# Two layers of local attention and feed-forward: another engine for the second x tile's statistics, a second DMA ring for the first weights, and the V halos on another engine

## The chip, the cores and the metric

The kernel runs on one core of a Trainium2 chip. The metric is the time of one execution on the device in microseconds. Each kernel was run several times. Kernels are compared only within the same rounds. The span in a profile starts a little later and ends a little earlier than the timed execution: 1228.4 us against 1230.1 us for the profiled run of the kernel before.

## The reference, cut to what matters

Two layers, each a sliding attention (32 heads of 32, window 8 with dilation 2) and a feed-forward part, with a layer norm ahead of both. x has 2048 rows of 1024, wqkv is 1024 x 3072, everything is bf16.

```python
def _layernorm(x, axis=-1, eps=1e-5):
    m = jnp.mean(x, axis=axis, keepdims=True)
    v = jnp.var(x, axis=axis, keepdims=True)
    return (x - m) / jnp.sqrt(v + eps)
# _A_ref: qkv = x @ wqkv, local attention, @ wo      _B_ref: gelu(x @ w1 + b1) @ w2 + b2
x = A_x
x = x + _A_ref(_layernorm(x, axis=-1), A_wqkv, A_wo)
x = x + _B_ref(_layernorm(x, axis=-1), B_w1, B_b1, B_w2, B_b2)
x = x + _A_ref(_layernorm(x, axis=-1), A_wqkv, A_wo)
x = x + _B_ref(_layernorm(x, axis=-1), B_w1, B_b1, B_w2, B_b2)
```

Nothing can be multiplied before the first rows of x are loaded, normalised and transposed. That start is what the change is about.

## The kernel before

The rows are cut into 16 tiles of 128, and four tiles make a group. For the first group the kernel loads x tiles 0 and 1, then Wq in four pieces of 512 KB (two row blocks each, "quarters" below) with x tiles 2 and 3 in between, all issued by SyncE:

```python
    def load_wq_piece(wt, k):
        sp.dma_start(wt[:, k % (KD // 2):k % (KD // 2) + 2, :], wqkv_v[:, k:k + 2, 0:D])

    load_x(0, 0, 2)
    wq_first = [wpool.tile([P, KD // 2, D], BF16, name="wt") for _ in range(2)]
    for k in range(0, KD, 2):
        load_wq_piece(wq_first[k // (KD // 2)], k)
        if k < 4:
            load_x(0, 2 + k // 2, 3 + k // 2)
    # ...
    act.activation(one[:], eps_t[:], ACT.Sqrt)      # ScalarE's first activation, behind a table load
```

TensorE first runs 14 warm-up matmuls. Meanwhile VectorE computes the statistics of tiles 0 and 1 and ScalarE the square roots; then both tiles are normalised and transposed on TensorE. The last two lines put tiles 2 and 3 behind, in program order:

```python
        stats(0)
        stats(1)
        xn0 = norm(0)
        xn1 = norm(1, (0, 2 * P, D))
        transpose_on_pe(xn0, xa[0][:, 0, :, :], [(0, 2, act.copy), (2, 8, act.copy)])
        transpose_on_pe(xn1, xa[0][:, 1, :, :], [(0, 2, vec.tensor_copy)])
        transpose_on_pe(xn1, xa[0][:, 1, :, :], [(2, 8, act.copy)])
        stats(2)
        stats(3)
        for tt in range(2, 4):
            first_late.append((norm(tt), xa[0][:, tt, :, :]))
```

The first Wq matmuls then work on the columns of tiles 0 and 1 alone, a Wq quarter at a time, and the transposes of tiles 2 and 3 are slipped in:

```python
        for kq in range(4 if n == 0 else 0):
            for c in range(7):
                first[c] = qkv_chunk(wq, c, xnT, first.get(c), kq * (KD // 4), (kq + 1) * (KD // 4), 0, 2)
                if (kq, c) == (2, 3):
                    transpose_on_pe(*first_late.pop(0), [(0, KD, act.copy)])
                # ... tile 3 at (3, 4)
```

The halo of V (the last 14 columns of the group before) is copied by ScalarE, except in the second group:

```python
                (act.copy if n > 1 else pool.tensor_copy)(vT[:, :, 0:HALO], st[n - 1]["vT"][:, :, T:T + HALO])
```

## Time and profile before

| | kernel before |
|---|---|
| time, median of 3 runs | 1230.35 us (1230.22 to 1230.75) |
| span in the profile | 1228.36 us |
| TensorE busy | 99% |
| x1 landed | 4.25 us |
| first Wq matmul issued | 8.26 us |
| x3 landed | 9.91 us |
| transposes of tile 2 | 12.24 us |
| last weight load of TensorE | 1224.96 us |
| last output landed | 1227.38 us |

Times inside a run count from the start of the span. TensorE is busy 99% of the span, so only what happens before its unbroken run of matmuls starts, or a wait that breaks this run, or the end behind the last matmul, can change the time. The lines of the profile are shown in the prediction. To compare two kernels I use one more reading: each trace has the same 5770 weight loads of TensorE in the same order, so the start of the k-th load in one trace minus that in the other tells how far TensorE is behind at that point. Where this difference steps, time was lost or won.

### The profile page before, as it was taken

To read this page: it belongs to the slowest core of one execution; us is meant where nothing else is said; L and a number is where in the kernel's file an instruction comes from. 1 tells how busy PE (TensorE), PEld (TensorE's weight loads), DVE (VectorE), ACT (ScalarE), POOL (GpSimd) and SP (SyncE) were. 2 spreads that over 40 slices of the span, in tenths; PEclk is the share of its full clock that TensorE was granted. 3 is DMA by queue.
4 is the path that set the end of the run, shared out by engine and by line. 5 is a ranking of instruction groups with operands and counts; after the bars stand their busy time and mean duration, and the time that the engine had idled before them with its cause. 6 is when DMAs were issued, how large, how long until landed. Compare 5 with 4: busy or idle time off the path is not lost.

```text
span 1228.4 us, 13955 instructions
## 1 busy us (share of the span) xinstructions
PE 1221.6 (99%) x5720; PEld 632.7 (52%) x5770; DVE 861.5 (70%) x912; ACT 315.6 (26%) x497; POOL 120.9 (10%) x219
## 2 busy tenths in 40 slices
PE   9999999999999999999999999999999999999998
PEld 7666544456444564446544465444654444444444
DVE  7999896998898999375993759937599797011001
ACT  5343253014310233202431024410244001300310
POOL 2330025010101101100001000000000002000000
PEclk9999999999999999999999999999999999999999
DMA  9965674766638645856557565576664558446441
GB/s 302 290 206 164 176 233 151 202 178 199 219 128 245 188 150 166 239 170 175 161 158 230 172 171 181 157 216 201 171 200 147 186 194 209 149 159 194 156 135 52
DMA packets 223647, 226.64 MB, mean 185 GB/s; under 512 B 71824, under 2 KB 190752, under 8 KB 221536
## 3 DMA queue, kind: packets, MB, share of 16 engines
q1 hardware_dynamic: 214704, 208.69, 56.3%
q0 software_dynamic: 8880, 17.07, 4.2%
q8 instruction: 45, 0.74, 0.2%
q14 instruction: 18, 0.15, 0.0%
HBM read 189.01 MB, written 4.19 MB: 157 GB/s over the span
## 4 chain that ended last, share of the span: by engine, by line
PE 99%; DVE 0%; issue 0%; DMA 0%
PE acc L117 99%; DMA x<-in_A_x_dram 0%; DVE stats L92 0%; PE acc L211 0%; DVE xn L92 0%; DVE x L92 0%; DVE mv L92 0%; DVE rstd L92 0%
## 5 line engine op out<-in xcount | busy, mean ns | idle before, releaser
L117 PE MATMUL acc<-xnT,wt 128*128 128x512 bf16 (+1 forms) x3392 | 720.3, 375 | 0.1
L117 PEld LDWEIGHTS <-wt 128*128 128x128 bf16 x3392 | 400.8, 120 | 317.4
L117 PE MATMUL acc<-wt,hT 128*128 128x512 bf16 (+1 forms) x1780 | 386.0, 376 | 2.1
L117 PEld LDWEIGHTS <-hT 128*128 128x128 bf16 x1820 | 178.1, 98 | 209.0
L92 DVE TENSOR_TENSOR big<-big 128x1024 bf16<-128x1024 bf16 (+2 forms) x184 | 244.8, 1359 | 2.2
L92 ACT ACTIVATE hT<-acc,b1T 128x512 bf16<-128x512 f32 x224 | 152.1, 687 | 325.9 <-PE acc L117 325.8
L92 DVE TENSOR_TENSOR big<-qT,kT 128x4096 bf16<-128x4096 bf16 x64 | 143.8, 2283 | 36.3 <-ACT kT L92 35.9
L92 DVE TENSOR_TENSOR big<-abc,vT 128x4096 bf16<-128x4096 bf16 x64 | 144.6, 2284 | 11.0 <-DMA abc<-a 7.1
L92 DVE TENSOR_TENSOR tmp<-acc,b2bc 128x512 f32<-128x512 f32 x56 | 38.6, 689 | 159.8 <-PE acc L117 156.7
L92 ACT CAST qT<-acc 128x512 bf16<-128x512 f32 (+1 forms) x72 | 38.0, 543 | 276.8 <-PE acc L117 274.6
L117 PE MATMUL acc<-wt,oT 128*128 128x512 bf16 x440 | 97.6, 379 | 0.4
L92 DVE BATCH_NORM_STATS2 stats<-x 128x6 f32<-128x512 bf16 x116 | 77.4, 681 | 6.0 <-DMA x<-in_A_x_dram 5.0
L117 PEld LDWEIGHTS <-oT 128*128 128x128 bf16 x448 | 43.8, 98 | 53.0 <-issue 0.3
L92 DVE TENSOR_TENSOR x<-acc,big 128x512 bf16<-128x512 f32 (+1 forms) x9 | 5.7, 632 | 90.0 <-PE acc L117 90.0
L92 POOL TENSOR_TENSOR rstd<-mv,eps_t 128x1 f32<-128x1 f32 x54 | 16.7, 308 | 524.2 <-DVE mv L92 524.2
L92 ACT CAST vT<-acc 128x512 bf16<-128x512 f32 x64 | 37.4, 585 | 101.9 <-PE acc L117 101.9
L92 ACT CAST kT<-acc 128x512 bf16<-128x512 f32 x64 | 37.3, 584 | 64.5 <-PE acc L117 64.5
L92 DVE TENSOR_TENSOR x<-acc,x 128x512 bf16<-128x512 f32 x64 | 42.9, 670 | 5.1 <-PE acc L117 4.7
L92 DVE TENSOR_SCALAR xn<-x,mv,rstd 128x1024 bf16<-128x1024 bf16 (+2 forms) x53 | 28.5, 540 | 20.1 <-POOL rstd L92 19.9
L92 DVE TENSOR_TENSOR x<-tmp,x 128x512 bf16<-128x512 f32 x56 | 38.6, 689 | 1.4
L92 POOL DMA_DIRECT2D big<-big x24 | 13.3, 563 | 212.5 <-DVE big L92 212.5
L92 ACT ACT_TABLE_LOAD x17 | 21.8, 1283 | 38.9 <-DVE e L92 30.5
(62 smaller groups left out, 285.4 us busy)
## 6 DMA issues: line engine op xcount, KB each, us to landing
wt<-in_B_w_dram SPq DMA_DIRECT2D x56, 1024.0 KB, 5.6
wt<-in_B_w_dram SPq DMA_DIRECT2D x64, 896.0 KB, 4.8
wt<-in_A_wqkv_dram SPq DMA_DIRECT2D x46, 1024.0 KB, 5.6
wt<-in_A_wo_dram SPq DMA_DIRECT2D x16, 1024.0 KB, 5.0
abc<-a POOLq DMA_DIRECT2D x32, 256.0 KB, 4.6
big<-big POOLq DMA_DIRECT2D x24, 256.0 KB, 3.8
x<-in_A_x_dram SPq DMA_DIRECT2D x16, 256.0 KB, 7.1
out_dram<-x SPq DMA_DIRECT2D x31, 128.0 KB, 1.8
```

What stands on the lines that cost most here:

```text
L92: inst = f(*args, **kwargs)
L117: return pe(nc.tensor.matmul(*args, **kwargs))
```

## The change

Its intent is a shorter start. The statistics of x tile 1 go to ScalarE, so that VectorE can normalise tile 0 at once; its reciprocal square root goes to GpSimd. Wq comes in eight row blocks of 256 KB, three of them through ScalarE's DMA ring (the queue of the transfers that this engine issues), the rest through SyncE's; x tiles 2 and 3 are asked for one Wq quarter later. All V halos are copied by GpSimd. The loads:

```diff
-    def load_wq_piece(wt, k):
-        sp.dma_start(wt[:, k % (KD // 2):k % (KD // 2) + 2, :], wqkv_v[:, k:k + 2, 0:D])
+    def load_wq_piece(wt, k, engine):
+        engine.dma_start(wt[:, k % (KD // 2), :], wqkv_v[:, k, 0:D])
 
     load_x(0, 0, 2)
     wq_first = [wpool.tile([P, KD // 2, D], BF16, name="wt") for _ in range(2)]
     for k in range(0, KD, 2):
-        load_wq_piece(wq_first[k // (KD // 2)], k)
-        if k < 4:
-            load_x(0, 2 + k // 2, 3 + k // 2)
-
+        load_wq_piece(wq_first[k // (KD // 2)], k, sp)
+        if 2 <= k < 6:
+            load_x(0, 1 + k // 2, 2 + k // 2)
+
+    load_wq_piece(wq_first[1], KD - 1, sp)
 # ... cut
+    act.on = True
     act.activation(one[:], eps_t[:], ACT.Sqrt)
+    act.on = True
+    for k in range(1, KD - 2, 2):
+        load_wq_piece(wq_first[k // (KD // 2)], k, act)
+    act.on = False
```

The statistics and the halos:

```diff
+            if tt == 0:
+                rstds[tt] = lnp.tile([P, 1], F32, name="rstd")
+                pool.tensor_tensor(out=rstds[tt][:], in0=mvs[tt][:, 1:2], in1=eps_t[:], op=ALU.add)
+                pool.tensor_tensor(out=rstds[tt][:], in0=rstds[tt][:], in1=mhalf[:], op=ALU.pow)
+            else:
+                act.activation(stds[tt][:], mvs[tt][:, 1:2], ACT.Sqrt, bias=eps_t[:])
+
+        def stats_on_act(tt):
 # ... cut: junk, less, mvs[tt] are allocated
+            act.activation(junk[:], x[tt][:], ACT.Identity, scale=-1.0 / D, accum_out=less[:])
+            act.activation(junk[:], x[tt][:], ACT.Square, bias=less[:], accum_out=mvs[tt][:, 1:2])
+            act.activation(stds[tt][:], mvs[tt][:, 1:2], ACT.Sqrt, scale=1.0 / D, bias=eps_t[:])
 # ... cut
         stats(0)
-        stats(1)
+        less = stats_on_act(1)
         xn0 = norm(0)
+        vec.tensor_scalar(out=mvs[1][:, 0:1], in0=less[:], scalar1=-1.0, scalar2=None, op0=ALU.mult)
         xn1 = norm(1, (0, 2 * P, D))
 # ... cut
-                (act.copy if n > 1 else pool.tensor_copy)(vT[:, :, 0:HALO], st[n - 1]["vT"][:, :, T:T + HALO])
+                pool.tensor_copy(vT[:, :, 0:HALO], st[n - 1]["vT"][:, :, T:T + HALO])
```

More of the change, by code (lines that the diff above doesn't have):

```diff
@@ L228, in ln_first @@
         mvs = {}
-        stds = {}
+        stds, rstds = {}, {}
         def stats(tt):
@@ L237, in stats @@
             stds[tt] = lnp.tile([P, 1], F32, name="std")
-            act.activation(stds[tt][:], mvs[tt][:, 1:2], ACT.Sqrt, bias=eps_t[:])
+            if tt == 0:
[5 more added lines that the diff above has]
+        def stats_on_act(tt):
+            junk = lnp.tile([P, D], BF16, name="xn", bufs=3)
+            less = lnp.tile([P, 1], F32, name="less")
+            mvs[tt] = lnp.tile([P, 2], F32, name="mv")
+            act.activation(junk[:], x[tt][:], ACT.Identity, scale=-1.0 / D, accum_out=less[:])
+            act.activation(junk[:], x[tt][:], ACT.Square, bias=less[:], accum_out=mvs[tt][:, 1:2])
+            stds[tt] = lnp.tile([P, 1], F32, name="std")
+            act.activation(stds[tt][:], mvs[tt][:, 1:2], ACT.Sqrt, scale=1.0 / D, bias=eps_t[:])
+            return less
         def norm(tt, bounds=(0, D)):
-            rstd = lnp.tile([P, 1], F32, name="rstd")
-            vec.reciprocal(rstd[:], stds[tt][:])
+            rstd = rstds.get(tt)
+            if rstd is None:
+                rstd = lnp.tile([P, 1], F32, name="rstd")
+                vec.reciprocal(rstd[:], stds[tt][:])
             xn = lnp.tile([P, D], BF16, name="xn", bufs=3)
```

## The prediction

> **What bounds the kernel now.** I read the page first: busy time by engine, then the chain that ended last.
>
> ```profile
> PE 1221.6 (99%) x5720; PEld 632.7 (52%) x5770; DVE 861.5 (70%) x912; ACT 315.6 (26%) x497; POOL 120.9 (10%) x219
> ...
> PE 99%; DVE 0%; issue 0%; DMA 0%
> ```
>
> TensorE is the bound, and it has next to nothing to give: 1228.4 - 1221.6 = 6.8 us of the span are without a matmul, of which 1.0 lies before the first one and about 3.1 after the last. In the view of waits by engine PE has one wait in the whole run, that first 1.0 us. In the long stages 49 matmuls of 512 columns are listed as 10.74 us; the 53 ns pauses between such groups come at regular distances and have no releaser, so I take them for missing records. So a gain can only lie in the first 15 us, before the matmuls run without a break. The chain of waits in the window 0 to 16 us (start, length, what) is the main view:
>
> ```profile
> 0.74 2.69 DMA x<-in_A_x_dram
> ...
> 3.46 1.30 DVE stats L92 x2
> ...
> 4.99 1.16 DVE stats L92 x2
> ...
> 6.44 0.55 DVE xn L92
> ...
> 7.10 0.74 DVE xn L92 x2
> 7.84 0.05 issue
> 7.89 0.51 PE acc L211 x6
> 8.40 4.01 PE acc L117 x36
> 12.41 0.45 PE acc L211 x8
> 12.85 1.75 PE acc L117 x16
> ```
>
> The reader is to see three things. Until 8.4 us VectorE leads: statistics of x tile 0, of x tile 1, then both normalisations, then the transposes (L211). From 8.26 us (issue of the first Wq matmul) PE runs on. And the transposes of tile 2 are due after 36 Wq matmuls, at 12.24 in the PE timeline; its xn was written at 11.53 + 0.55 = 12.07. That is a margin of 0.17 us only. The third view is the stretches with their DMA share (the last two columns):
>
> ```profile
> 3.50:4.50 1.00, 1.00 (x4) 0.42 (x3) 1.00 (x2) 0.00 (x0) 0.00 (x0) 1.00 0.91 227
> 4.50:5.50 1.00, 1.00 (x4) 0.34 (x3) 0.97 (x4) 0.29 (x1) 0.00 (x0) 1.00 0.89 234
> ...
> 8.20:12.20 4.00, 4.00 (x40) 3.96 (x38) 3.48 (x10) 1.87 (x4) 0.00 (x0) 1.00 1.05 395
> ```
>
> The DMA engines are full in this stage too, at 395 GB/s once the first microseconds are over, so the order in which bytes are asked for is the order in which tiles come. 256 KB (one x tile or one Wq row block) take 0.262/395 = 0.66 us.
>
> **What the Trainium skill says.** "DMA: Bandwidth & Descriptors", section Issuing engines are not separate DMA queues: transfers started on several engines share the same 16 DMA engines, and only the sequencer's issue time is saved. Its section Queues, rings and completion order has each DMA engine take turns between the rings with work. The trace before agrees with the shared limit (share 1.05 above); it has no second hardware ring at work here, so the turns are untested. "ScalarE: Activation LUTs", section What ACT_TABLE_LOAD costs: an activation takes about 186 ns + 0.833 ns an element, 280 with a pointer as bias: 1039 and 1133 ns for 1024. The trace has 1.06 and 1.15 us for just these two forms. "TensorE: Matmul & The Clock Gate", Part 1: the array starts at half clock and needs about 3.4 us of work. The trace agrees in kind: the 14 warm-up matmuls are spaced 427 ns, the transposes right after them 56 ns.
>
> **The change part by part.**
>
> 1. **Tile 0.** rstd goes from ScalarE and a reciprocal to two GpSimd operations, and the statistics of tile 1 leave VectorE. The GpSimd pair with VectorE quiet:
>
> ```profile
> 14.93 0.19 POOL L92 TENSOR_TENSOR rstd<-mv,eps_t 128x1 f32<-128x1 f32 x1 [13.07 <-DVE mv L92]
> 15.20 0.56 POOL L92 TENSOR_TENSOR rstd<-rstd,mhalf 128x1 f32<-128x1 f32 x1
> ```
>
> mv is done at 4.99; + 0.09 to the start, 0.27 to the next start, 0.56: rstd at 5.91. Normalising from 5.95 takes 0.55: xn0 at 6.50 and not 6.99, 0.49 earlier. But PE is in its warm-up until 6.95 (last of 14 issued at 6.52, 0.43 each), and the warm-up is unchanged. The first transpose moves from 7.05 to 6.95 at best: 0.1 us, and it is not the last input.
>
> 2. **Tile 1.** ScalarE now does its statistics. The same operations later in the run:
>
> ```profile
> 27.33 1.06 ACT L92 ACTIVATE xn<-x 128x1024 bf16<-128x1024 bf16 x1
> 28.29 0.19 ACT L92 ACTIVATION_READ_ACCUMULATOR xn<-x 128x1 f32 x1
> 28.51 1.15 ACT L92 ACTIVATE xn<-x,less 128x1024 bf16<-128x1024 bf16 x1
> 29.57 0.19 ACT L92 ACTIVATION_READ_ACCUMULATOR xn<-x,less 128x1 f32 x1
> ```
>
> That is 29.76 - 27.33 = 2.43 us to the variance. x1 lands at 4.25 (the landing recorded for its transfer). Start 4.27, variance 6.70, square root 0.03 + 0.29: 7.02; signal and reciprocal 0.05 + 0.11: 7.18; first 256 columns of xn1 0.04 + 0.35: 7.57. Before, they were there at 7.44. So this part is slower by 0.13 us: VectorE needed 1.44 us for what ScalarE takes 2.43. From those columns to the first Wq matmul it was 8.26 - 7.44 = 0.82 us, by the rest of the normalisation (0.47) and the copy of the transposes on VectorE (0.29), unchanged. First Wq matmul: 8.39. If Wq blocks on the second ring take turns with the end of x1, x1 is later by up to some 0.3 us, and the first matmul at 8.7.
>
> 3. **Order of the loads.** Before: x0 x1 w01 x2 w23 x3 w45 w67. In units of 256 KB x3 was the 8th and landed at 9.91; the 10th (w45) at 11.27, the 12th at 12.62. Now SyncE asks for x0 x1 w0 w2 x2 w4 x3 w6 w7 and ScalarE for w1 w3 w5. With turns taken, x3 is behind both x, w0 to w5 and x2: again the 10th unit, 11.2 to 11.3. VectorE works in program order: statistics of tile 2, statistics of tile 3, then norm 2. From the landing of x3 to the end of xn2 it took 12.07 - 9.91 = 2.16 us. So xn2 at 11.25 + 2.16 = 13.41, its transposes at 13.46. PE gets there at 8.39 + 3.96 = 12.35 and waits about 1.1 us. Against 12.24 before that is + 1.2 us. It isn't added to the delay of part 2 but swallows it. Tile 3 follows 0.65 us behind tile 2 and PE needs 2.2 us between them: no second wait.
>
> What was to be gained is small: Wq held PE once, 30 ns before the third quarter (landed 11.265, due at 11.24).
>
> 4. **V halos.** Five copies of 0.28 us leave ScalarE (26% busy). On GpSimd the one such copy of before took 2.18 us beside VectorE:
>
> ```profile
> 85.69 2.18 POOL L92 COPY vT<-vT 128x112 bf16<-128x112 bf16 x1
> ```
>
> The V evictions on ScalarE run at their 1.73 us beat before, during and after it, so nothing waits for it but the weighted sum, first at 89.6 us, and later halos have over 15 us until then. VectorE may lose 2 us a halo to the shared port at worst; it has 30% to spare. Effect on PE: 0.
>
> Sum: - 0.1 to + 0.4 from parts 1 and 2, swallowed by + 1.2 from part 3 if x3 comes as the 10th; + 0.1 to + 0.6 if the ring of ScalarE gets a smaller share or two rings fill the slow microseconds 3.5 to 5.5 (227 GB/s) better.
>
> **The rivals.**
> - *The start gets shorter.* The most that can be won is between the end of the warm-up and the first Wq matmul: 8.26 - 6.95 = 1.3 us, of which 16 transposes need 0.9; so 0.4 us at most. Against it: ScalarE's chain ends after VectorE's old one. Time 1229.9 to 1230.3. Chance 0.15.
> - *ScalarE is blocked by its own transfers.* In the trace before, SyncE's later transfers wait for earlier ones to land (3.8 us in four waits for Wq). If one issued on ScalarE has to wait so, the statistics of tile 1 behind it start late: 1 us for one such wait, 3 for two. Against it: ScalarE has from 2.24 (end of its first activation) to 4.25 for three issues of some 0.45 us. Time 1231.5 to 1234. Chance 0.12.
> - *It is hidden:* x3 comes by 10.1, and the result is + 0.1 to + 0.4. Chance 0.25.
> - *GpSimd in program order holds a halo behind other work and stalls the matmuls.* The even beat of the evictions above speaks against it. A few us at most; chance 0.03.
>
> **Range and chances.** The main path (about 0.45) gives + 0.6 to + 1.3; the rivals spread from - 0.4 to + 3. The weighted middle is near + 0.8: 1231.2. Runs of the kernel before lie 0.5 us apart. I take 1230.0 to 1232.6. Two per cent are 25 us, and no part comes near it: within 2% 0.985, slower 0.01, faster 0.005.
>
> **What would show it.** Step 1: xn0 at about 6.5, transposes not before 6.95. Step 2: ScalarE's first activation on x1 at 4.3 to 4.6, xn1's first columns at 7.5 to 7.9, first Wq matmul at 8.4 to 8.7. Step 3: a wait of VectorE for x3 until about 11.2 and a PE gap of about 1 us before the transposes of tile 2; from there an even shift to the end. Step 4: no gap in PE after 15 us. The prediction is wrong if that gap is missing (then x3 came earlier than the order of bytes says), or if PE loses or gains anything after 15 us.

## The result, and the profile after

The changed kernel took 1231.78 us (median of 6 runs, 1231.66 to 1231.96), the kernel before in the same rounds 1230.29 us (6 runs, 1230.14 to 1230.75). The ratio is 1.0012 with a 95% interval of 0.9999 to 1.0025: the same within 2%. A ratio here is the mean time of one kernel's fast runs over the mean of the other's of the same rounds, so it is not quite the ratio of the medians. The interval is too wide to tell 1.5 us from nothing by itself, but each of the six runs is above each of the six of the kernel before, and the traces account for the difference: the profiled spans are 1228.36 and 1229.82 us, 1.46 apart.

The page of the changed kernel, in its busy time by engine, its queues and its chain that ended last:

```profile
PE 1222.9 (99%) x5770; PEld 632.4 (51%) x5770; DVE 860.7 (70%) x909; ACT 316.6 (26%) x495; POOL 129.7 (11%) x226
...
q10 hardware_dynamic: 432, 0.79, 0.2%
...
PE 99%; DMA 0%; ACT 0%; DVE 0%; SPq 0%; issue 0%
```

TensorE is the bound as before. The queue q10 is new: it is ScalarE's ring, and its 0.79 MB are the three Wq row blocks. Of the 9 us more of GpSimd (129.7 against 120.9) some 6 are the change's: five more halos (4.12 us and four times 0.28) and two rstd operations (0.75); the rest I did not trace.

The chain of waits of the changed kernel in the window 0 to 16 us (start, length, what):

```profile
1.20 4.19 DMA x<-in_A_x_dram
5.38 0.02 issue
5.41 1.16 ACT xn L92 x2
...
6.59 1.25 ACT xn L92 x2
...
7.86 0.30 ACT std L92
...
8.38 0.74 DVE xn L92 x2
...
9.69 3.99 PE acc L117 x36
13.68 0.45 PE acc L217 x8
14.12 1.75 PE acc L117 x16
```

The start now hangs on x1. Its transfer is asked for at 1.20 us, as before, but lands at 5.38 and not at 4.25. ScalarE's statistics follow with the lengths that it takes everywhere, the first Wq matmul is issued at 9.55 and not at 8.26, and nothing breaks the row after that: 36 Wq matmuls, then tile 2's transposes at once (9.69 + 3.99 = 13.68 in this view).

The stretches of the changed kernel, with PEclk, DMA share and GB/s as the last three columns:

```profile
3.50:4.50 1.00, 1.00 (x5) 0.45 (x4) 0.90 (x2) 0.00 (x0) 0.00 (x0) 1.00 1.04 387
4.50:5.50 1.00, 1.00 (x6) 0.29 (x3) 0.59 (x2) 0.10 (x1) 0.21 (x2) 1.00 1.05 395
```

The DMA engines moved 387 and 395 GB/s here against 227 and 234 before. So the transfers as a whole were faster; only x1 was later. The timeline of ScalarE says why (ACTq is its sequencer, which issues transfers):

```profile
0.91 1.34 ACTq L92 DMA_DIRECT2D wt<-in_A_wqkv_dram  x3
2.03 0.20 ACT L92 ACTIVATE one<-eps_t 128x1 f32<-128x1 f32 x1
5.41 1.06 ACT L92 ACTIVATE xn<-x 128x1024 bf16<-128x1024 bf16 x1 [3.17 <-DMA x<-in_A_x_dram]
```

In program order the activation stands ahead of the three transfers. It started at 2.03, behind its table load, but the transfers were issued from 0.91 on. So in this trace ScalarE's sequencer went on while the activation still waited for its turn. w1 was asked for 0.3 us before x1, and w3 (at 1.32) right after it, on a ring of their own; w1 landed at 4.73, before x1.

Where the 1.46 us came from, by the shift of TensorE's weight loads:

| place | shift of the step |
|---|---|
| first Wq matmul, 8.26 to 9.55 us | +1.29 |
| third Wq quarter: the 0.02 us wait of before is gone | -0.02 |
| 124.4 us, first Wo matmuls: a gap between two weight loads is shorter by this | -0.065 |
| end: behind the last weight load; 0.24 of it from the last output's landing to the end of the span, 0.98 to 1.23 us | +0.25 |
| sum | +1.455 |

The cause of the gap at 124.4 us is open: before, two weight loads there started 0.37 us apart and not 0.22, the profile names no releaser, and VectorE had written the last oT column 0.44 us earlier. The fourth row was a surprise. In the trace, once the last output has landed, SyncE checks further completion counters, one every 0.061 us: two of them before, six after.

### The profile page after: what moved, and what is told of

It reads as the page before. It is cut to its first block, busy times and chain, and to the rows that moved or that the text cites. A ratio compares the mean times of both kernels' runs of the same rounds, so it can differ in the third digit from the quotient of the medians.

```text
span 1229.8 us, 14017 instructions
## 1 busy us (share of the span) xinstructions
PE 1222.9 (99%) x5770; PEld 632.4 (51%) x5770; DVE 860.7 (70%) x909; ACT 316.6 (26%) x495; POOL 129.7 (11%) x226
## 4 chain that ended last, share of the span: by engine, by line
PE 99%; DMA 0%; ACT 0%; DVE 0%; SPq 0%; issue 0%
PE acc L117 99%; DMA x<-in_A_x_dram 0%; ACT xn L92 0%; PE acc L217 0%; DVE xn L92 0%; DVE x L92 0%; SPq L92 0%; ACT std L92 0%; DVE rstd L92 0%
## 5 line engine op out<-in xcount | busy, mean ns | idle before, releaser
L92 POOL DMA_DIRECT2D abc<-a x32 | 17.6, 558 | 135.7 <-DVE a L92 135.6
```

Source lines behind the costliest of these rows:

```text
L92: inst = f(*args, **kwargs)
```

## The experiments

Eleven variants were run, and a twelfth at the end. All gave correct results; all were timed over five rounds. By its times each is the same as the kernel before within 2%, and no interval of a ratio excludes 1, so the readings rest on the traces, and the times only check them. Each variant has one profile, and the spans of nine runs of the kernel before in one group already went from 1228.0 to 1229.5 us: a step of a few tenths in one trace shows where time went in that execution, and not that it goes there each time.

| run | this, us | before, us | ratio (95%) | span | x1 landed | first Wq matmul | tile 2 transposes |
|---|---|---|---|---|---|---|---|
| before, first profile | 1230.35 | | | 1228.36 | 4.25 | 8.26 | 12.24 |
| the change | 1231.78 | 1230.29 | 1.0012 (0.9999 to 1.0025) | 1229.82 | 5.38 | 9.55 | 13.51 |
| loads_only | 1230.64 | 1230.32 | 1.0003 (0.9991 to 1.0016) | 1228.73 | 5.09 | 8.52 | 12.48 |
| stats_only | 1230.84 | 1230.32 | 1.0005 (0.9993 to 1.0018) | 1228.69 | 4.07 | 8.24 | 12.65 |
| halos_only | 1230.11 | 1230.32 | 0.9999 (0.9986 to 1.0011) | 1228.67 | 4.10 | 8.29 | 12.73 |
| x1_on_act_ring | 1231.06 | 1230.32 | 1.0006 (0.9992 to 1.0019) | 1229.11 | 4.76 | 8.92 | 12.88 |
| w_held | 1232.26 | 1230.63 | 1.0012 (0.9998 to 1.0026) | 1230.12 | 4.02 | 8.19 | 13.82 |
| w_held_dve | 1231.94 | 1230.63 | 1.0009 (0.9997 to 1.0022) | 1229.60 | 4.27 | 8.45 | 13.38 |
| one_ring | 1231.66 | 1230.63 | 1.0008 (0.9996 to 1.0021) | 1229.76 | 4.21 | 8.38 | 13.54 |
| one_ring_turned | 1230.90 | 1230.34 | 1.0005 (0.9992 to 1.0017) | 1228.75 | 4.13 | 8.30 | 12.26 |
| x_halves_turned | 1230.99 | 1230.34 | 1.0012 (0.9999 to 1.0024) | 1228.65 | 4.24 | 8.47 | 12.43 |
| turned_late_halves | 1230.34 | 1230.53 | 0.9998 (0.9985 to 1.0012) | 1228.19 | 4.16 | 8.32 | 12.29 |

(more_transfers and one_ring_touch are told below.) The theory after the first comparison was: ScalarE's early Wq transfers delay x1, and ScalarE's chain, which starts only when x1 is there, passes the whole delay on. The rivals: the chain on ScalarE is itself too long; or the order of loads alone does it.

### The three parts alone

**loads_only.** The kernel before with the loads of the change, statistics and halos as before.

```diff
-        load_wq_piece(wq_first[k // (KD // 2)], k)
-        if k < 4:
-            load_x(0, 2 + k // 2, 3 + k // 2)
+        load_wq_piece(wq_first[k // (KD // 2)], k, sp)
+        if 2 <= k < 6:
+            load_x(0, 1 + k // 2, 2 + k // 2)
+    # ... and w1, w3, w5 by ScalarE, w7 by SyncE, as in the change
```

> The kernel before with the new loads alone (Wq row blocks from two rings, x tiles 2 and 3 later; statistics and halos as before). Theory A, the blocks on ScalarE's ring take turns with x1 and delay it: x1 again lands at about 5.4 us and not 4.25. VectorE's statistics of tile 1 then end at 5.40 + 1.44 + 0.03 = 6.87, the first columns of xn1 are written at about 7.95 and the first Wq matmul issues at about 8.8 (+ 0.5 us). With the end of the program 0.25 us longer (four transfers more, see the tail of the trace after): 1230.29 + 0.5 + 0.25 = 1231.0. Rival B, the delay of x1 is of no account because the statistics on ScalarE are what costs: first Wq matmul at 8.3, total 1230.5 at most.

x1 landed 0.84 us later than in the kernel before (5.09), but the first Wq matmul was issued only 0.26 later (8.52). Two lines of its chain of waits, window 0 to 16:

```profile
1.19 3.90 DMA x<-in_A_x_dram
...
5.11 1.30 DVE stats L92 x2
```

With the statistics on VectorE the delay is cushioned: in the kernel before, VectorE is at tile 0 until 4.99 and could not have begun tile 1 when it landed at 4.25. So some 0.6 us of the 0.84 cost nothing here. Tile 2's transposes came without a gap.

**stats_only.** The kernel before with the statistics of the change, loads and halos as before.

```diff
         stats(0)
-        stats(1)
+        less = stats_on_act(1)
         xn0 = norm(0)
+        vec.tensor_scalar(out=mvs[1][:, 0:1], in0=less[:], scalar1=-1.0, scalar2=None, op0=ALU.mult)
 # ... and rstd of tile 0 by GpSimd, as in the change
```

> The kernel before with the new statistics alone (tile 1 on ScalarE, rstd of tile 0 on GpSimd; loads and halos as before). Theory A: x1 lands at 4.25 as before, ScalarE's chain takes 2.43 + 0.32 us, first Wq matmul at about 8.4 (+ 0.13), no other change: 1230.4. Rival B, the ScalarE chain is the loss: first Wq matmul at 9 or later, 1231.2 or more.

With x1 undelayed (4.07), ScalarE's statistics ran from 4.10 to 6.52 and the first Wq matmul was issued at 8.24, 0.02 before that of the kernel before. ScalarE's longer chain costs nothing here, because it starts 0.9 us before VectorE's would. The span is 0.33 longer all the same, mainly by one wait of TensorE. Its timeline:

```profile
11.72 1.09 PE L117 MATMUL acc<-xnT,wt 128*128 128x256 bf16 x8 [0.22 <-DMA wt<-in_A_wqkv_dram]
```

That is the wait for the third Wq quarter, which landed at 11.67 instead of 11.27; the matmul was issued 0.42 later than it would have been in an even row. (The timeline's 0.22 counts from the modelled end of the matmul before.) Another 0.06 us was lost at 58 us and 0.13 won at 124.4 us. The loads are the same as before, so I take this for a difference from run to run: this stretch of transfers was slower, 154 and 217 GB/s in 3.5 to 5.5 us.

**halos_only.** One line.

```diff
-                (act.copy if n > 1 else pool.tensor_copy)(vT[:, :, 0:HALO], st[n - 1]["vT"][:, :, T:T + HALO])
+                pool.tensor_copy(vT[:, :, 0:HALO], st[n - 1]["vT"][:, :, T:T + HALO])
```

> The kernel before with the V halos on GpSimd alone. Theory A: no change of the first 15 us; one wait at the first Wo matmuls shorter by 0.06 us at most; 1230.2 to 1230.3. Rival C, GpSimd's halos stall the matmuls or the end of the program: a shift of PE anywhere after 60 us, or a longer tail; 1230.5 or more.

The first Wq matmul was issued at 8.29, and the same wait for the third quarter, 0.45 us, appeared here too (it landed at 11.75): again a run-to-run matter of the old loads, not of the halos. TensorE has no other new wait. The longest halo of the changed kernel, in the timeline of GpSimd:

```profile
121.37 4.12 POOL L92 COPY vT<-vT 128x112 bf16<-128x112 bf16 x1 [29.55 <-DVE big L92]
```

It took 4.12 us beside VectorE's large products and 4.12 in halos_only as well (120.61 to 124.73), while four later ones took 0.28. Nothing waited for it. So the halos are neutral, and the three parts alone give +0.26, -0.02 and +0.03 us at the first Wq matmul, but +1.29 together. The effects don't add: the loads delay x1, and the statistics on ScalarE take away the cushion.

### When and where the Wq blocks are asked for

**x1_on_act_ring.** The change, with x1 as the first transfer of ScalarE's ring, ahead of w1.

```diff
-    load_x(0, 0, 2)
+    load_x(0, 0, 1)
 # ...
     act.on = True
+    act.dma_start(x[1][:], x_in[P:2 * P, :])
     for k in range(1, KD - 2, 2):
```

> The changed kernel with x tile 1 loaded by ScalarE's ring ahead of its three Wq blocks, x0 by SyncE's ring. Theory A, it is the turns between rings that made x1 late: x0 and x1 share the engines and both land at about 4.2, ScalarE's chain ends 2.75 us later, first Wq matmul at 8.4 to 8.6 and not 9.55; 1230.6 to 1230.9, that is 0.9 to 1.2 below the changed kernel. Rival D, ScalarE is late for another reason (its queue is held by the transfers it issues): first Wq matmul stays above 9.2, 1231.5 or more.

x1 landed at 4.76 and the first Wq matmul came at 8.92, so 0.63 of the 1.29 us was regained, not all: x1 still shares the engines with x0 and w0 of the other ring, and x0 was later too (4.10 against 3.43). The trace also has the event that the prediction's second rival feared: w5, the ninth transfer of the program, was issued by ScalarE only at 4.12, just behind the landing of x0, the first (4.10), and kept ScalarE's sequencer until 4.46. It cost nothing, since x1 landed later still.

**w_held.** The change, with ScalarE's transfers held until its first activation is done at 2.24: that activation now writes a column of w1's tile, so w1's transfer has to wait for it.

```diff
-    act.activation(one[:], eps_t[:], ACT.Sqrt)
+    act.activation(wq_first[0][:, 1, 0:1], eps_t[:], ACT.Sqrt)
```

> The changed kernel with ScalarE's three transfers held until its first activation is done (2.24 us and not 0.91), all else as changed. Theory A, x1 is late because Wq blocks that were asked for before it run beside it: x1 lands at 4.1 to 4.4, the variance is ready 2.43 us later, first Wq matmul at 8.2 to 8.5 instead of 9.55, no wait for Wq or for tile 2 after it; 1230.4 to 1230.7, at least 1 us below the changed kernel. Rival E, x1 is late because two rings share the engines whenever the blocks come: x1 at 5 or later, first Wq matmul at 9.2 or later.

This is the prediction's own picture of the change: Wq on ScalarE's ring from 2.24 on. x1 landed at 4.02, and the first Wq matmul was issued at 8.19, 1.36 us before that of the change and even 0.07 before that of the kernel before. The timeline of ScalarE:

```profile
2.04 0.21 ACT L92 ACTIVATE wt<-eps_t 128x1 bf16<-128x1 f32 x1
2.27 1.35 ACTq L92 DMA_DIRECT2D wt<-in_A_wqkv_dram  x3
4.04 1.06 ACT L92 ACTIVATE xn<-x 128x1024 bf16<-128x1024 bf16 x1 [1.80 <-DMA x<-in_A_x_dram]
```

That settles the cause of the +1.29: it is that ScalarE's Wq transfers were asked for from 0.91 to 1.80, around x1 at 1.20, and not from 2.27 on. But the run as a whole is no faster than the change, and its expected total (1230.4 to 1230.7) was missed. One of its stretches, and its timeline of TensorE:

```profile
4.50:5.50 1.00, 1.00 (x5) 0.33 (x4) 0.38 (x2) 0.97 (x3) 0.42 (x2) 1.00 0.60 213
```

```profile
13.82 0.62 PE L217 MATMUL acc<-ident,xn 128*128 128x128 bf16 x8 [1.51 <-DVE xn L92]
```

The transfers were slow again (213 GB/s at a share of 0.60), x3 landed at 11.60 and not at 10.13, and TensorE waited for tile 2: its transposes came 1.58 us later than in the kernel before. This is the gap that the prediction expected of the change.

**w_held_dve.** The same hold on loads_only (statistics on VectorE).

```diff
-    act.activation(one[:], eps_t[:], ACT.Sqrt)
+    act.activation(wq_first[0][:, 1, 0:1], eps_t[:], ACT.Sqrt)
```

> The loads of the change held in the same way, but with the statistics and halos of the kernel before. Theory A: x1 at 4.1 to 4.4 again, which VectorE does not need before 4.9, so first Wq matmul at 8.25 as before; with the quarters of Wq no longer waited for and the tail 0.25 longer: 1230.2 to 1230.5, equal to w_held within 0.2. That would say that the statistics on ScalarE win nothing when x1 is in time and lose a microsecond when it is late.

x1 landed at 4.27, x3 at 11.16, tile 2's transposes came at 13.38, 1.14 later than before, against 0.24 later in loads_only. The gap is a matter of the loads, whichever engine does the statistics. The total expected, without this gap, was missed here too (1231.94).

**one_ring.** The change with all blocks on SyncE's ring, in the order in which the prediction had them land: x0 x1 w0 w1 w2 w3 x2 w4 w5 x3 w6 w7.

```diff
-    for k in range(0, KD, 2):
+    for k in range(KD):
         load_wq_piece(wq_first[k // (KD // 2)], k, sp)
-        if 2 <= k < 6:
-            load_x(0, 1 + k // 2, 2 + k // 2)
-    load_wq_piece(wq_first[1], KD - 1, sp)
+        if k in (3, 5):
+            load_x(0, 2 + k // 5, 3 + k // 5)
 # ... and no transfers by ScalarE
```

> The changed kernel with all Wq row blocks from SyncE's ring in the order x0 x1 w0 w1 w2 w3 x2 w4 w5 x3 w6 w7. Theory A: x1 at 4.1 to 4.3 and first Wq matmul at 8.2 to 8.4. Theory G, it is the second ring that fills the DMA engines between 3.5 and 6.5 us: here the rate falls to 150 to 280 GB/s again, x3 lands at 11.2 to 11.8 as the 10th block, xn2 2.2 us later, and PE waits 1.0 to 1.5 us before the transposes of tile 2, as predicted for the change; 1231.4 to 1232. Rival H, the smaller blocks fill them and not the second ring: about 390 GB/s, x3 at about 10.2, no such wait; 1230.4 to 1230.6.

Lines of its chain of waits, and one of its stretches:

```profile
5.19 6.13 DMA x<-in_A_x_dram
...
11.34 1.30 DVE stats L92 x2
...
12.94 0.56 DVE xn L92
...
13.54 0.62 PE acc L214 x8
```

```profile
3.50:4.50 1.00, 1.00 (x4) 0.42 (x3) 0.93 (x2) 0.26 (x1) 0.00 (x0) 1.00 1.02 215
```

Without a second ring everything falls where the prediction had put it: first Wq matmul at 8.38 (8.39 predicted), x3 at 11.32 (11.25), xn2 done at 13.48 (13.41), tile 2's transposes 1.30 us late (+1.2). So the prediction described this kernel closely, and it isn't the one that was made. The smaller blocks alone (rival H) do not fill the slow microseconds.

### The end of the run

**more_transfers.** The change, with five later x loads in halves: five transfers more, the same bytes.

```diff
-            sp.dma_start(x[t][:], x_in[t * P:(t + 1) * P, :])
+            cuts = (0, HALF, D) if NTT <= t < NTT + 5 else (0, D)
+            for lo, hi in zip(cuts[:-1], cuts[1:]):
+                sp.dma_start(x[t][:, lo:hi], x_in[t * P:(t + 1) * P, lo:hi])
```

> The changed kernel with five later x loads in two halves each, 9 transfers more than the kernel before in place of 4. Theory F, the tail depends on the number of transfers by turns of eight, since SyncE checks eight completion marks in a fixed order at the end, some 0.06 us each, and only those behind the last transfer's mark cost time: 6 checks after the last landing become 1, the tail 0.3 us shorter, all else as in the changed kernel: 1231.4 to 1231.5. Rival: the 0.25 us longer tail of the changed kernel comes of something else; then no change, 1231.8.

1231.54 us against 1230.63 (ratio 1.0009), span 1229.32, first Wq matmul at 9.45. After the last landing (1228.41) there was one check, and the span ended 0.91 us after it, against 1.23 with six checks in the change and 0.98 with two in the kernel before. The counts fit a fixed round of eight counters: each transfer more moves the last one on by a place, so 2 checks become 6 with four transfers more (2 - 4 + 8) and 1 with nine more (2 - 9 + 8). So the 0.24 us behind the last landing of the change come from the number of its transfers, not from what they carry. w_held, w_held_dve, loads_only, x1_on_act_ring and one_ring, which have four more than the kernel before like the change, all show six checks as well.

### Can the pieces be put together to win?

**one_ring_turned.** one_ring with tile 2 normalised before the statistics of tile 3, which takes tile 2's transposes out of the wait for x3; and the five halved x loads for the end.

```diff
-        stats(2)
-        stats(3)
         for tt in range(2, 4):
+            stats(tt)
             first_late.append((norm(tt), xa[0][:, tt, :, :]))
 # ... and load_x in halves as in more_transfers
```

> The kernel of the run one_ring with two edits: VectorE normalises tile 2 before it takes the statistics of tile 3, and five later x loads come in halves (the shorter tail). Theory A: in one_ring PE waited 1.3 us for xn2 because its normalisation stood behind the statistics of tile 3, which came last; now xn2 needs x2 alone (9.3 us + 1.5 + 0.3 + 0.2 + 0.55 = 11.9), before PE gets there at 12.3, and xn3 is written by 14.4, just as PE needs it. The wait goes, and the tail is 0.3 shorter: 1.4 to 1.6 us under one_ring and 0.1 to 0.4 under the kernel before. Rival: PE waits for Wq or tile 3 instead, and most of the 1.3 us stay.

The gap was gone: xn2 was done at 11.83 and the transposes came at 12.26. Those of tile 3 came 0.15 us late. The span fell by 1.0 us against one_ring, but not below the kernel before, because a new wait had come up at 58 us, at the start of the second group. Its timeline of TensorE there:

```profile
59.13 1.08 PE L117 MATMUL acc<-xnT,wt 128*128 128x512 bf16 x4 [0.21 <-DMA wt<-in_A_wqkv_dram]
```

A 1-MB weight block landed at 59.09, 57.24 in the kernel before. TensorE was 0.44 us further behind from there on (0.17 to 0.60 by the weight loads).

**x_halves_turned.** As one_ring_turned, but x0 and x1 first, in halves over both rings, and then w1 and w3 on ScalarE's ring.

```diff
-    load_x(0, 0, 2)
+    sp.dma_start(x[0][:, 0:HALF], x_in[0:P, 0:HALF])
+    sp.dma_start(x[1][:, 0:HALF], x_in[P:2 * P, 0:HALF])
 # ...
+    act.dma_start(x[0][:, HALF:D], x_in[0:P, HALF:D])
+    act.dma_start(x[1][:, HALF:D], x_in[P:2 * P, HALF:D])
+    for k in range(1, KD - 4, 2):
+        load_wq_piece(wq_first[k // (KD // 2)], k, act)
```

> Both rings from the start, but with nothing ahead of or beside the first two x tiles: each of x0 and x1 in two halves, one per ring, then w0 w2 x2 w4 w5 x3 w6 w7 on SyncE's and w1 w3 on ScalarE's; tile 2 normalised before the statistics of tile 3; nine transfers more than the kernel before. Theory A (order of bytes, both rings full): x0 at 3.4 to 3.6, x1 at 4.1 to 4.4, first Wq matmul 8.2 to 8.5, no wait after it, short tail: 0.1 to 0.4 us under the kernel before. Rival: Wq's bytes come as slowly as in one_ring and w_held (213 to 295 GB/s between 3.5 and 6.5 us) and a wait for Wq or tile 2 of 0.3 us or more remains.

x1 landed at 4.24, no earlier than on one ring, and the first Wq matmul came at 8.47. The wait at 58 us was there too (the block landed at 58.90; three more x loads were in halves here). Two of its five runs were over 1232 us. No gain.

**one_ring_touch.** Why are the transfers fast with two rings? One idea was that something has to be touched first: this is one_ring_turned with a 32-KB read of the first columns of w0 by ScalarE at 0.91, whose result is not used (and four halved loads instead of five).

```diff
     act.activation(one[:], eps_t[:], ACT.Sqrt)
+    early_w = const.tile([P, P], BF16, name="early_w")
+    act.dma_start(early_w[:], wqkv_v[:, 0, 0:P])
```

> one_ring_turned with one more small transfer: ScalarE asks at 0.91 us for the first 128 columns of w0 (32 KB, used by nobody). Question: what makes the DMA engines slow between 3.5 and 6.5 us in every kernel whose Wq blocks come after the x tiles, and fast where ScalarE asked for Wq at 0.91. Theory I, the first reads of Wq are slow whenever they come: with this early read the rate from 3.5 to 6.5 is 380 to 400 GB/s and w7 lands at about 11.5. Theory J, it takes a second ring with much work: the rate stays at 210 to 350 and w7 at 12.5 to 13. The time differs little from one_ring_turned: 0 to 0.3 us.

1231.02 us against 1230.34 (ratio 1.0006), span 1229.35, first Wq matmul at 8.45, and 305, 246 and 367 GB/s in the three slow microseconds, not the 380 to 400 of theory I. one_ring_turned, without the small read, had 285, 318 and 373, so the idea is not supported. The wait at 58 us cost 0.77 us here. The rates of all runs, in GB/s:

| run | ScalarE's ring | 3.5 to 4.5 us | 4.5 to 5.5 us | 5.5 to 6.5 us |
|---|---|---|---|---|
| before | none | 227 | 234 | 330 |
| stats_only | none | 154 | 217 | 279 |
| halos_only | none | 209 | 227 | 207 |
| one_ring | none | 215 | 285 | 346 |
| one_ring_turned | none | 285 | 318 | 373 |
| turned_late_halves | none | 174 | 322 | 338 |
| one_ring_touch | 32 KB at 0.91 | 305 | 246 | 367 |
| w_held | Wq from 2.24 | 250 | 213 | 295 |
| w_held_dve | Wq from 2.24 | 332 | 240 | 330 |
| x_halves_turned | x halves, then two Wq blocks | 338 | 211 | 395 |
| x1_on_act_ring | x1, then three Wq blocks, from 0.91 | 402 | 387 | 389 |
| loads_only | three Wq blocks from 0.91 | 404 | 391 | 399 |
| the change | three Wq blocks from 0.91 | 387 | 395 | 410 |
| more_transfers | three Wq blocks from 0.91 | 397 | 406 | 408 |

Only with several whole blocks on ScalarE's ring from 0.91 on are these three microseconds full. Why is left open.

**turned_late_halves.** The last run asks where the wait at 58 us of the turned kernels comes from. The same as one_ring_turned, but with the five extra transfers late in the run, where nothing waits for them.

```diff
-            cuts = (0, HALF, D) if NTT <= t < NTT + 5 else (0, D)
-            for lo, hi in zip(cuts[:-1], cuts[1:]):
-                sp.dma_start(x[t][:, lo:hi], x_in[t * P:(t + 1) * P, lo:hi])
+            sp.dma_start(x[t][:], x_in[t * P:(t + 1) * P, :])
 # ... in gen_ffn2
-                sp.dma_start(wt[:], w2_v[:, kq * KQ:(kq + 1) * KQ, cols])
+                cuts = (0, 4, KQ) if n == 3 and dh * 4 + kq < 5 else (0, KQ)
+                for lo, hi in zip(cuts[:-1], cuts[1:]):
+                    sp.dma_start(wt[:, lo:hi, :], w2_v[:, kq * KQ + lo:kq * KQ + hi, cols])
```

> one_ring_turned with its five extra transfers moved: the x loads of groups 1 and 2 are whole again, and five W2 loads of the second layer's group 3 (first at some 700 us) come in halves instead. Theory (the wait of one_ring_turned at 58.4 us comes from the halved x loads: SyncE spends about 0.5 us on each issue, the tiles of groups 1 and 2 land later, so the DMA transposes behind them on SyncE and the Wk block behind those are late; it landed at 59.09 there, at 57.24 in the kernel before and 57.46 in one_ring): no PE wait at 58.4 us, the block lands by 57.6; first Wq matmul 8.2 to 8.4, no wait before tile 2, 1 check at the end, span 1228.1 to 1228.4, time within 0.3 us of the kernel before and perhaps 0.2 below it. Rival (the turn of the normalisations itself delays VectorE's later tiles): the block lands after 58.4 and PE waits 0.3 to 0.7 us there again, span 1228.6 or more.

The block landed at 56.48, and TensorE's timeline shows an unbroken row there:

```profile
56.70 4.48 PE L117 MATMUL acc<-xnT,wt 128*128 128x512 bf16 x20
```

So without the halved x loads the wait was gone, as the theory said; in one_ring_turned SyncE issued the x loads of the last group from 37.14 on, here from 35.51. more_transfers points the same way: it differs from the change by the halves alone, and its block landed at 57.48 us against 56.60. But the halves are not the only thing that makes the block late: in stats_only and halos_only, with whole x loads but slow first transfers (the last Wq quarter landed at 13.0 and 13.1, at 12.6 before), it landed at 58.97 and 58.77. How much of the wait of one_ring_turned was due to the halves, one profile of each can't tell. The span is 1228.19, 0.16 below the first profile of the kernel before; of this 0.06 comes from one check less at the end, and the rest from TensorE (+0.06 at the first Wq matmul, -0.02 at the third Wq quarter, -0.15 at 124.4 us). The time is 1230.34 against 1230.53 us, ratio 0.9998. It has the shortest span of the variants and is still the same as the kernel before. No version found beats it by anything that the times could show.

## Why the prediction was right or wrong

**The total was right, by another road than the one described.** The prediction said about +0.8 us (1231.2), with a main path of +0.6 to +1.3; it is +1.49 by the medians, above that path but inside the whole range. But its main step did not happen, and another step, put down as small, was as large.

**Bound.** Right. TensorE ran almost without a gap from its first Wq matmul on, and 1.29 of the 1.46 us are the shift of the start. The share of 1.05 that the prediction took as agreeing with a limit shared by several issuing engines came from one ring, so it could not test that; with two at work from 3.5 to 6.5 us in the change, the share was 1.04 to 1.07.

**Part 1, tile 0.** xn0 was done at 6.62, and 6.50 was predicted. That the first transpose could not come before the end of the warm-up at 6.95 was wrong, but without effect: the warm-up was shorter in this run. Its matmuls went from 427 to some 215 ns apart at about 4.0 us, so that tile 0's transposes came at 6.67 (6.51 in stats_only). In the kernel before all 14 had kept the slow pace. The 14 matmuls are the same in all kernels, and the pace doubled between 3.5 and 3.9 us in stats_only, between 5.7 and 6.1 in one_ring_touch and not within the 14 in the kernel before, so this moment differs from run to run.

**Part 2, tile 1: here is the failed step.** The lengths were right: ScalarE took 5.41 to 7.83, 2.42 us where 2.43 was predicted, and stats_only (8.24) and one_ring (8.38) put the first Wq matmul where this part had it, 8.39. Wrong was its last sentence, "If Wq blocks on the second ring take turns with the end of x1, x1 is later by up to some 0.3 us, and the first matmul at 8.7." The mechanism was named and its size missed: x1 was 1.13 us later, and the first matmul came at 9.55. The reason is in the rival on ScalarE's own transfers, "ScalarE has from 2.24 (end of its first activation) to 4.25 for three issues": the issues were taken to start after the activation. They started at 0.91. Turns were thus taken over all of x1's transfer and not over its last part: from the landing of x0 at 3.58 to that of x1 it was 1.80 us, at 387 to 395 GB/s some 0.70 MB by an estimate from these figures, that is 0.44 MB beside x1's own 0.26, more than w1 alone. w_held, which makes that assumption true, has x1 at 4.02.

**Part 3, order of the loads.** The wait of TensorE for tile 2 was predicted as about 1.1 us, and the change doesn't have it. By its own criterion ("wrong if that gap is missing (then x3 came earlier than the order of bytes says)") this part failed. The order was right, for x3 was again the 10th to land, but the bytes before it flowed faster: x3 landed at 10.13, not at 11.25, as two rings at work from 0.91 filled the microseconds between 3.5 and 6.5. The sum had listed that as "two rings fill the slow microseconds 3.5 to 5.5 (227 GB/s) better" and gave it less weight. Besides, TensorE was 1.29 us late by then, so that even VectorE's later end of xn2 (12.84) left 0.7 us before the transposes at 13.51. one_ring and w_held show that the mechanism itself is real: 1.30 and 1.58 us.

So one cause, asking for Wq at 0.91 on a second ring, switched the two steps: it made x1 late and x3 early. That the two sizes, +1.27 observed and +1.2 predicted at tile 2, are so close is chance.

**Part 4, the halos.** Right: no effect on TensorE. The worst case for VectorE, 2 us a halo, did not show: beside the longest halo (4.12 us) four of its products took 3.56 us, as in the kernel before. The copy itself was the one that took longer.

**Missed.** The end of the run, +0.25 us. The prediction expected "an even shift to the end"; four transfers more cost four more checks. And the -0.065 at 124.4 us, behind the first 15 us, after which the prediction expected no change. Both are small against the start.

**The rivals.** A shorter start: no, in no run by more than 0.07. ScalarE blocked by its own transfers: no; ScalarE stood idle for 3.17 us for x1, and its issues were over at 2.25. Hidden: its premise came true (x3 by 10.1), its result of +0.1 to +0.4 did not, because it too left the delay of x1 small. GpSimd stalls: no.

## What to carry to other kernels

A transfer that stands behind a computation in an engine's program may be issued long before that computation starts (at 0.91 against 2.03 us here), so a second DMA ring can take its share ahead of the one tile that the start waits for: order the first transfers across both rings, and read their issue times from the trace. Judge two parts of a change together where one delays an input and the other takes away the slack that would have hidden it (+0.26 and -0.02 us alone, +1.29 together). And a total that agrees proves no mechanism; look for the gap that the reasoning names, in the place that it names.

## What the Trainium skill lacked or had wrong

- "DMA: Bandwidth & Descriptors", section Issuing engines are not separate DMA queues, says that starting transfers on several engines saves only the sequencer's time to initiate them. Here three Wq blocks on ScalarE's ring from 0.91 us on went with 387 to 404 GB/s between 3.5 and 4.5 us, against 154 to 285 with everything on SyncE's ring, and x3 as the 10th block landed at 10.13 instead of 11.32. With the same three blocks on that ring from 2.27 on (w_held) it was 250. The runs don't settle why.
- The same page, section Queues, rings and completion order, has the engines take turns between rings. The runs agree, and add what this costs a tile: x1, 256 KB asked for at 1.20, landed at 5.38 (5.28 in more_transfers, 5.09 in loads_only) with Wq on the other ring from 0.91, and between 4.02 and 4.27 in the profiles where it had none before 2.24.
- No page that I read says that the end of a run depends on the number of transfers before it: checks of 0.061 us each, one, two or six of them, 0.91, 0.98 and 1.23 us from the last landing to the end.
